# A spectral filter and an MLP on one core: constant tables moved from SyncE's queue into GpSimd's, and four copies and a weight preparation redistributed between two engines

## The chip, the core and the metric

The kernel runs on one core of one Trainium2 chip. The metric is the device time of one execution in microseconds (us); lower is better. The kernel before has a median of 833.29 us over three runs (833.17, 833.29 and 837.02). One further execution was recorded by the profiler; its times are given on their own below.

## What is computed

Eight sequences of 3008 rows with 256 channels are filtered along the rows by a real FFT, a multiplication with a complex filter and the inverse FFT. The 24064 filtered rows then pass through an MLP with 2048 hidden units and the activation h + sin²(alpha·h)/alpha.

```python
# x [8, 3008, 256]; filt_r, filt_i [1505, 256]; w_in [256, 2048]; w_out [2048, 256]
X = np.fft.rfft(x, axis=1)
Y = X * (filt_r + 1j * filt_i)[None]
y = np.fft.irfft(Y, n=3008, axis=1).reshape(24064, 256)
h = y @ w_in
g = h + np.sin(alpha * h) ** 2 / (alpha + 1e-09)
out = g @ w_out
```

## The kernel before, in words

**The transform.** 3008 is 47 times 64, so each transform is two small matrix products with constant tables: a first one over 47 points (table wa), a second one over 64 points (table wb), the product with the filter, and the same two steps backwards with the tables wg (64 points) and we (47 points). All tables are constants of the program and lie in device memory.

**Batches 1 to 7** run woven into the MLP. Their steps (f1, f2x, product, f2g, f3) are put by hand into `plan`, a table of half slots, and between steps the data are reordered by way of device memory, in SyncE's DMA queue. The MLP works on 47 chunks of 512 rows: `mlp_in` (L274), a sine on ScalarE (L276), `square` on VectorE (L281), `mlp_out` (L293), with two `mlp_in` blocks to each of the eight slots of a chunk.

**Batch 0** has nothing to hide behind, so it is done ahead of the MLP, in an order written out by hand (L496 to L505), and reordered on the chip: TensorE multiplies by the identity and the result is copied out of PSUM. Its steps are:

- `f1_chip` (L151): the first forward half; PSUM goes to a_c, half by ScalarE and half by VectorE.
- `turn1` (L162): reorders a_c into bint. `f2x` (L201): the second forward half, with wb; ScalarE copies it to xs.
- `fold_filter` (L405): VectorE copies the filter rows 0 to 63 of fri to rows 64 to 127, 8 of the 24 frequency groups at a time. `product` (L210): VectorE multiplies xs with the two parts of the filter into z and t2, four groups at a time (k = 0 to 5).
- `g_chip` (L172): the first backward half, for one k and one half of the channels: eight matmuls, four of z with wg and four of t2 with a second table, wgs, one after the other in one PSUM tile of 128x512. The copy to b_c is ScalarE's, and VectorE's for the very last tile (k = 5, half 1).
- `turn2` (L183): reorders b_c into gin, two rows at a time. j = 0 to 3 run ahead of the MLP, where ScalarE takes j = 0 and 2 and VectorE 1 and 3; the other twelve lie in the first four slots.
- `f3` (L249): the second backward half into yt, for groups G = 0 and 1 and channel blocks cb = 0 and 1 ahead of the MLP. L264 copies the columns of this chunk, by VectorE for (0, 1) and ScalarE for the other three; L267 copies what belongs to the next chunk, always by VectorE.

z and t2 have two buffers, xs four. PSUM tiles come from three pools: psf (tag f, three), psh (tag ph, three), pso (tag po, two). `keep_busy` (L388) issues matmuls with zeros, so that TensorE isn't idle.

**Loads.** GpSimd issues every transfer that casts float32 to float16, in one queue: x of batch 0 in eight transfers (L134; four parts of 80 and of 14 partitions each), the filter in twelve (L397 and L401: three sets s0 = 0, 8, 16 with two transfers for the real and two for the imaginary part), w_in in four (L479), then x of batch 1 in eight and w_out in two (L348). The first filter transfer waits until part 1 of x has landed. SyncE issues the tables that need no cast, in its own queue, and each waits for a landing:

```python
gate(nc.sync.dma_start(out=wb[:, 8 * 128:], in_=wb_d.ap()[:, 8 * 128:]), x_dma[0, 2])
for s0 in (0, 8, 16):
    cs = slice(128 * s0, 128 * s0 + 1024)
    gate(nc.sync.dma_start(out=wg[:, cs], in_=wg_d.ap()[:, cs]), filter_dma[s0, 0])
    nc.sync.dma_start(out=wgs[:, cs], in_=wgs_d.ap()[:, cs])
```

`filter_dma[s0, 0]` is the second transfer of the real part of set s0. Each piece of wg and of wgs serves two of the six k. The first 8 of the 24 column blocks of wb come early and ungated.

**Weights.** `prep_w_out` (L351) scales the sixteen blocks of w_out by 1/alpha on VectorE, four blocks a call, in slots 6, 8, 10 and 12 of the plan. `mlp_out` of chunk 0 begins in slot 8 and uses the blocks in order.

Of the kernel before, what the change touches and what calls it, by code (L numbers as in the profile page):

```python
# [9 lines left out]
FP16 = mybir.dt.float16  # L10
# [54 lines left out]
def kernel(  # L65
# [10 lines left out]
    nc = tc.nc  # L76
# [51 lines left out]
    def load_x(b, parts=2):  # L128

        xt[b] = (xbpool if b else vpool).tile([GT, RP, C], FP16, name="xt", tag="xb" if b else "vt")  # L130
        n = RP // parts
        for h in range(parts):
            for p0, p1 in ((0, 80), (80, GT)):
                x_dma[b, h] = nc.gpsimd.dma_start(  # L134
                    out=xt[b][p0:p1, n * h:n * h + n, :],
                    in_=dram(x, (b * S + RP * p0 + n * h) * C, [[RP * C, p1 - p0], [1, n * C]]))
# [32 lines left out]
        (nc.vector.tensor_copy if t in (1, 3, 5, 7) else nc.scalar.copy)(  # L169
            out=bint[0][:, 2 * t:2 * t + 2, :], in_=ps)  # L170

    def g_chip(k, half):  # L172

        ps = (psh if half else pso).tile([128, 4, 128], FP32, name="psg0", tag="ph" if half else "po")
        for i in range(4):
            for v, w in ((z, wg), (t2, wgs)):
                nc.tensor.matmul(out=ps[:, i, :], lhsT=v[k][:, i, 128 * half:128 * half + 128],
                                 rhs=w[:, 128 * (4 * k + i):128 * (4 * k + i) + 128],
                                 start=(v is z), stop=(v is t2))
        (nc.vector.tensor_copy if k == 5 and half else nc.scalar.copy)(  # L180
            out=b_c[:, half, :, 4 * k:4 * k + 4, :], in_=ps.rearrange("p s (r a) -> p r s a", a=4))

    def turn2(j):  # L183

        ps = (psf if j < 4 else pso).tile([4 * NK, 2, C], FP32, name="pst2", tag="f" if j < 4 else "po")
        rows = b_c.rearrange("p h r s a -> p h r (s a)")
        for i in range(2):
            for half in range(2):
                nc.tensor.matmul(out=ps[:, i, 128 * half:128 * half + 128],
                                 lhsT=rows[:, half, 2 * j + i], rhs=ident, start=True, stop=True)  # L190
        (nc.scalar.copy if j in (0, 2) or j > 4 and j % 3 == 1 else nc.vector.tensor_copy)(  # L191
            out=gin[0][:, 2 * j:2 * j + 2, :], in_=ps)

    def shuffle1(b):
# [54 lines left out]
    def f3(G, cb):  # L249


        b, a = divmod(G, 8)
        g, lo = divmod(GT * G, 128)
        n = min(GT, 128 - lo)
        if cb == 0:
            if lo == 0 or G == 0:
                yt[g] = ypool.tile([128, 2, 4, 128], FP16, name="yt", tag="yt")
            if n < GT:
                yt[g + 1] = ypool.tile([128, 2, 4, 128], FP16, name="yt", tag="yt")
        ps = psf.tile([128, 4, GT], FP32, name="psy", tag="f")  # L260
        for t in range(4):
            nc.tensor.matmul(out=ps[:, t, :], lhsT=gin[b][:, 4 * a + t, 128 * cb:128 * cb + 128],  # L262
                             rhs=we if b else we2, start=True, stop=True)
        (nc.vector.tensor_copy if G == 0 and cb else nc.scalar.copy)(  # L264
            out=yt[g][:, cb, :, lo:lo + n], in_=ps[:, :, 0:n])
        if n < GT:
            nc.vector.tensor_copy(out=yt[g + 1][:, cb, :, 0:GT - n], in_=ps[:, :, n:GT])  # L267
# [81 lines left out]
                                   in_=moe_w_out[1024 * h:1024 * h + 1024, :].rearrange("(b p) c -> p b c", p=128))  # L349

    def prep_w_out(k):  # L351
        for i in range(4 * k, 4 * k + 4):
            nc.vector.tensor_scalar(out=w_out2[:, i, :], in0=w_out16[:, i, :],  # L353
                                    scalar1=recip[:, i:i + 1], scalar2=None, op0=ALU.mult)

# [59 lines left out]
    def at(slot, f, *args):  # L415
        plan.setdefault(int(2 * slot), []).append((f, args))
# [19 lines left out]
    for g in range(NCH - 1):  # L436
# [4 lines left out]
        slots = (4, 6) if len(todo) == 2 else (3, 4, 6, 7) if g == 4 else (3, 4, 5, 6)  # L441
        for q, u in zip(slots, todo):
            at(8 * g + q, f3, *u)
    for k in range(4):
        at(6 + 2 * k, prep_w_out, k)
    for k in range(2):
        at(13, prep_m, k)
    at(14, load_w_in32, 0)
# [10 lines left out]
    with tc.manual_schedule():  # L459
        nc.sync.dma_start(out=wa2, in_=wa2_d.ap())  # L460
        nc.sync.dma_start(out=ident, in_=id_d.ap())
        nc.scalar.dma_start(out=alpha_r, in_=moe_alpha.rearrange("(a p) -> a p", p=128))
        nc.scalar.dma_start(out=ident32, in_=id32_d.ap())
        nc.scalar.dma_start(out=we2, in_=we2_d.ap())
        nc.scalar.dma_start(out=wa, in_=wa_d.ap())
        nc.scalar.dma_start(out=we, in_=we_d.ap())
        nc.sync.dma_start(out=wb[:, 0:8 * 128], in_=wb_d.ap()[:, 0:8 * 128])
        zero = cpool.tile([128, 512], FP16, name="zero")
        nc.vector.memset(zero, 0.0)
        warm = cpool.tile([128, 1], FP32, name="warm")  # L470
        nc.vector.memset(warm, 0.0)
        nc.scalar.activation(out=warm, in_=warm, func=AFT.Sin)
        load_x(0, 4)
        for s0 in (0, 8, 16):
            load_filter(s0, 8, None if s0 else x_dma[0, 1])
        for h in range(2):
            hs = slice(1024 * h, 1024 * h + 1024)
            for cb in range(2):
                w_in_dma[h, cb] = nc.gpsimd.dma_start(out=w_in16[:, cb, hs],  # L479
                                                      in_=moe_w_in[128 * cb:128 * cb + 128, hs])  # L480
        wgs = ginpool.tile([128, NK * 128], FP16, name="wgs", tag="gin")
        gate(nc.sync.dma_start(out=wb[:, 8 * 128:], in_=wb_d.ap()[:, 8 * 128:]), x_dma[0, 2])
        for s0 in (0, 8, 16):
            cs = slice(128 * s0, 128 * s0 + 1024)
            gate(nc.sync.dma_start(out=wg[:, cs], in_=wg_d.ap()[:, cs]), filter_dma[s0, 0])
            nc.sync.dma_start(out=wgs[:, cs], in_=wgs_d.ap()[:, cs])
        a_c = vpool.tile([128, 2, NK, 128], FP16, name="a_c", tag="vt")
        prep_alpha()
        keep_busy(8, zero)
        for k in range(8):  # L490
            f1_chip(k)
            if k % 2:
                keep_busy(2 if k < 7 else 1, zero)
        bint[0] = xbpool.tile([128, NK, C], FP16, name="bint", tag="xb")
        b_c = agpool.tile([128, 2, RP, NK, 4], FP16, name="b_c", tag="ag")
        for f, *args in (  # L496
                (turn1, 0), (turn1, 1), (turn1, 2), (f2x, 0, 0), (turn1, 3), (turn1, 4), (f2x, 0, 1),
                (turn1, 5), (turn1, 6), (f2x, 0, 2), (turn1, 7), (fold_filter, 0, 8), (turn1, 8),
                (f2x, 0, 3), (product, 0, 0, 0), (turn1, 9), (f2x, 0, 4), (turn1, 10), (f2x, 0, 5),
                (product, 0, 1, 0), (turn1, 11), (f2x, 0, 6), (keep_busy, 2, zero), (g_chip, 0, 0), (g_chip, 0, 1), (f2x, 0, 7),  # L500
                (fold_filter, 8, 8), (f2x, 0, 8), (keep_busy, 2, zero), (product, 0, 2, 0), (g_chip, 1, 0), (g_chip, 1, 1),
                (f2x, 0, 9), (keep_busy, 2, zero), (product, 0, 3, 0), (f2x, 0, 10), (f2x, 0, 11), (keep_busy, 2, zero), (g_chip, 2, 0), (g_chip, 2, 1),
                (fold_filter, 16, 8), (keep_busy, 2, zero), (product, 0, 4, 0), (g_chip, 3, 0), (g_chip, 3, 1),
                (product, 0, 5, 0), (keep_busy, 2, zero), (g_chip, 4, 0), (g_chip, 4, 1), (keep_busy, 2, zero), (g_chip, 5, 0), (g_chip, 5, 1),
                (keep_busy, 1, zero)):  # L505
            f(*args)
        gin[0] = ginpool.tile([4 * NK, RP, C], FP16, name="gin", tag="gin")
        for j in range(4):
            turn2(j)
        load_x(1, 4)  # L510
        load_w_out(0)
        load_w_out(1)
        for i in range(4):
            if i % 2 == 0:
                keep_busy(1, zero)
            f3(i // 2, i % 2)

        for g in range(NCH):
            for q in range(8):
                if g and q == 7:  # L520
                    evict_out(g - 1, 0)
                mlp_in(g, 2 * q)
                if g:
                    mlp_out(g - 1, q, 1)
                for f, args in plan.get(16 * g + 2 * q, ()):
                    f(*args)
                mlp_in(g, 2 * q + 1)
                if g:
                    mlp_out(g - 1, q, 0)
                for f, args in plan.get(16 * g + 2 * q + 1, ()):  # L530
                    f(*args)
                if g and q == 7:
                    evict_out(g - 1, 1)
                    store_out(g - 1, 0, 4, (nc.sync,))
                if q % 2:
                    square(g, q)
        out_last(NCH - 1)
# [28 lines left out]
```

## Time and profile before

| what | value |
|---|---|
| median of three runs | 833.29 us (833.17, 833.29, 837.02) |
| the profiled execution | 836.87 us, of which the span of instructions is 835.0 us |
| TensorE (PE) busy | 816.3 us, 98% of the span |
| VectorE (DVE), ScalarE (ACT), GpSimd (POOL) busy | 509.9, 619.0 and 35.0 us |
| PE busy from 120 to 800 us | 680.0 of 680 us |
| PE busy from 0 to 50 us | 36.9 of 50 us |
| last copy into b_c (batch 0) ends | 39.31 us |
| first mlp_in matmul | 42.23 us |
| mean granted clock of TensorE | 0.998 |

Times within the profile count from the start of the span. A row of the timeline names start and length, the engine, the line of the kernel and what is written from what; in square brackets stands how long the engine was idle before and what ended that wait. A row of the chain of waits names start, length and the piece of work which the end of the program hangs on. The queue q0 (software_dynamic) is the one that GpSimd issues, q1 (hardware_dynamic) the one of SyncE and ScalarE.

### The profile page before, as it was taken

Reading aid. Unit: us, or ns where it says so; the run is one execution under the profiler, and the core shown is the slowest. Engines: PE = TensorE matmul, PEld = TensorE weight load, DVE = VectorE, ACT = ScalarE, POOL = GpSimd, SP = SyncE. Lnnn points to the kernel's source line nnn. Section 1 sums busy time; section 2 is a strip of 40 time slices with the busy share of each in tenths; the row PEclk is TensorE's granted clock in tenths of the full one; section 3 lists DMA queues with packets and bytes.
Section 4 is the critical chain, followed back from the end, with each engine's and each line's share of the span. In section 5 each row is a group of like instructions: output and inputs, shape, how many; then the busy total and the mean of one; then the engine's idle time right before and its main releaser. Section 6 shows DMA issues by size and latency. Waiting matters only on the chain.

```text
span 835.0 us, 15131 instructions
## 1 busy us (share of the span) xinstructions
PE 816.3 (98%) x6242; PEld 573.1 (69%) x6242; DVE 509.9 (61%) x675; ACT 619.0 (74%) x1156; POOL 35.0 (4%) x65
## 2 busy tenths in 40 slices
PE   7699999999999999999999999999999999999997
PEld 4557776677767776677767776677766777766666
DVE  4586976676466665566655684567655775444442
ACT  5596987787777777788777887777877787766663
POOL 5400000000000000000000000000000000000000
PEclk9999999999999999999999999999999999999999
DMA  9946365424543164612834146331645123310111
GB/s 198 210 75 215 120 169 127 141 76 107 145 107 122 51 156 95 202 31 72 191 99 140 51 105 172 101 102 51 160 118 142 61 93 95 67 51 26 26 52 51
DMA packets 67829, 91.28 MB, mean 109 GB/s; under 512 B 5512, under 2 KB 52376, under 8 KB 66248
## 3 DMA queue, kind: packets, MB, share of 16 engines
q1 hardware_dynamic: 59664, 70.99, 29.5%
q0 software_dynamic: 7568, 19.14, 11.8%
q8 instruction: 49, 0.80, 0.4%
q10 hardware_dynamic: 528, 0.18, 0.1%
q14 instruction: 20, 0.16, 0.1%
HBM read 59.62 MB, written 46.66 MB: 127 GB/s over the span
## 4 chain that ended last, share of the span: by engine, by line
PE 91%; DMA 3%; DVE 3%; ACT 1%; POOL 1%; issue 0%; SPq 0%; POOLq 0%; DVEq 0%
PE po L293 42%; PE ph L274 37%; PE psa L143 3%; PE psy L262 3%; PE psg L234 2%; PE psx L204 2%; DMA fri<-in_filt_r_dram 1%; DMA wgs<-wgs_tbl 1%; PE pe L307 1%; DMA xt<-in_x_dram 1%; DVE vt L281 1%; PE psm L372 0%; ACT vt L276 0%; DVE gin L191 0%; DVE w_ina L385 0%
## 5 line engine op out<-in xcount | busy, mean ns | idle before, releaser
L276 ACT ACTIVATE vt<-ph 128x512 f16<-128x512 f32 x688 | 404.5, 601 | 141.8 <-PE ph L274 136.9
L293 PE MATMUL po<-w_out,vt 128*128 128x256 f16 x2944 | 426.5, 272 | 1.1 <-DVE w_out L353 0.6
L293 PEld LDWEIGHTS <-vt 128*128 128x128 f16 x2944 | 287.4, 98 | 172.2 <-issue 1.1
L274 PE MATMUL ph<-yt,w_ina 128*128 128x512 f16 x1376 | 399.4, 379 | 0.0
L281 DVE TENSOR_TENSOR vt<-vt 128x2048 f16<-128x2048 f16 x188 | 230.1, 1224 | 195.3 <-ACT vt L276 194.4
L274 PEld LDWEIGHTS <-w_ina 128*128 128x128 f16 x1376 | 128.2, 98 | 32.6
L318 DVE COPY ot<-po 128x512 f32<-128x512 f32 x92 | 62.9, 688 | 22.2 <-PE po L293 21.3
L208 ACT CAST xs<-psx 128x512 f16<-128x512 f32 x96 | 56.8, 596 | 7.6 <-PE psx L204 7.4
L144 DVE CAST asb<-psa 96x512 f16<-96x512 f32 x56 | 38.3, 685 | 33.4 <-PE psa L143 30.6
L236 ACT CAST gsb<-psg 128x512 f16<-128x512 f32 x84 | 49.5, 589 | 11.5 <-PE psg L234 10.7
L293 PE MATMUL po<-m_t,yt 128*128 128x256 f16 x368 | 55.2, 273 | 0.0
L267 DVE CAST yt<-psy 128x240 f16<-128x240 f32 (+45 forms) x92 | 32.2, 351 | 32.8 <-ACT yt L264 31.6
L264 ACT CAST yt<-psy 128x376 f16<-128x376 f32 (+46 forms) x127 | 45.9, 362 | 7.5 <-PE psy L262 0.6
L276 ACT ACTIVATE vt<-ph,alpha_t 128x512 f16<-128x512 f32 x64 | 43.7, 703 | 9.4 <-PE ph L274 9.3
L262 PE MATMUL psy<-we,gin 96*128 96x94 f16 x512 | 42.1, 204 | 0.0
L134 POOL DMA_DIRECT2D xt<-in_x_dram x40 | 21.3, 540 | 491.8 <-PE psy L262 300.7
L262 PEld LDWEIGHTS <-gin 96*128 96x128 f16 x512 | 35.6, 97 | 6.9 <-issue 0.5
L293 PEld LDWEIGHTS <-yt 128*128 128x128 f16 x368 | 36.0, 98 | 4.2
L144 ACT CAST asb<-psa 96x512 f16<-96x512 f32 x56 | 32.9, 587 | 8.0 <-PE psa L143 7.7
L217 DVE TENSOR_TENSOR z<-xs,fri 128x1024 f16<-128x1024 f16 x48 | 33.0, 687 | 8.3 <-ACT xs L208 4.6
L274 PE MATMUL ph<-yt,w_in 128*128 128x512 f16 x128 | 37.8, 379 | 0.2 <-ACT yt L264 0.2
L204 PE MATMUL psx<-bint,wb 128*128 128x256 f16 x192 | 36.8, 276 | 0.4 <-ACT bint L169 0.2
(69 smaller groups left out, 383.7 us busy)
## 6 DMA issues: line engine op xcount, KB each, us to landing
scr<-asb SPq DMA_DIRECT2D x14, 768.0 KB
bint<-scr SPq DMA_DIRECT2D x21, 512.0 KB
scr<-gsb SPq DMA_DIRECT2D x21, 512.0 KB
out_dram<-ot SPq DMA_DIRECT2D x31, 320.0 KB
xt<-in_x_dram POOLq DMA_DIRECT2D x12, 640.0 KB, 7.7
gin<-scr SPq DMA_DIRECT2D x7, 768.0 KB
out_dram<-ot SPq DMA_DIRECT2D x16, 256.0 KB
gin<-scr SPq DMA_DIRECT2D x7, 576.0 KB
```

The costliest lines, as they stand in the source:

```text
L144: (nc.vector.tensor_copy if u % 2 else nc.scalar.copy)(out=asb[b][:, 2 * u:2 * u + 2, :], in_=ps)
L204: nc.tensor.matmul(out=ps[:, i, :], lhsT=wb[:, 128 * (2 * t + i):128 * (2 * t + i) + 128], rhs=bint[b][:, 2 * t + i, :], start=True, stop= ...
L208: nc.scalar.copy(out=xs[b, t // 2][:, t % 2 * 2:t % 2 * 2 + 2, :], in_=ps)
L217: nc.vector.tensor_tensor(out=z[k], in0=xs[b, k], in1=fri[:, 0, k4, :], op=ALU.mult)
L236: nc.scalar.copy(out=gsb[b][:, 2 * t:2 * t + 2, :], in_=ps)
L262: nc.tensor.matmul(out=ps[:, t, :], lhsT=gin[b][:, 4 * a + t, 128 * cb:128 * cb + 128], rhs=we if b else we2, start=True, stop=True)
L264: (nc.vector.tensor_copy if G == 0 and cb else nc.scalar.copy)(out=yt[g][:, cb, :, lo:lo + n], in_=ps[:, :, 0:n])
L274: nc.tensor.matmul(out=ph, lhsT=(w_in16 if g < 4 else w_ina)[:, cb, 128 * jb:128 * jb + 128], rhs=yt[g][:, cb], start=(cb == 0), stop=(cb ...
L276: nc.scalar.activation(out=vt[g][:, jb, :], in_=ph, func=AFT.Sin, scale=alpha_t[:, jb:jb + 1] if g < 4 else 1.0)
L281: nc.vector.tensor_tensor(out=v4, in0=v4, in1=v4, op=ALU.mult)
L293: nc.tensor.matmul(out=po[g, h][:, i, :], lhsT=vt[g][:, k, ts] if k < 16 else yt[g][:, k - 16, t], rhs=w_out2[:, k, :] if k < 16 else m_t[ ...
L318: nc.vector.tensor_copy(out=ot[g][:, 2 * h:2 * h + 2, :], in_=po[g, h])
```

## The change

It makes five edits.

1. The seven late tables (the rest of wb, three pieces of wg and three of wgs) are issued by GpSimd instead of SyncE, without gates, each set right behind the filter set of the same s0. w_in is issued behind all of them.
2. The last backward tile of batch 0, `g_chip(5, 1)`, becomes two PSUM tiles of two blocks each; VectorE copies the first and ScalarE the second. One of the two zero matmuls ahead of `g_chip(5, 0)` goes.
3. `turn2` with j = 3 is copied by ScalarE, so that ScalarE has three of the first four and VectorE one.
4. The main copies of `f3` ahead of the MLP alternate: VectorE has cb = 0 of both groups, ScalarE cb = 1.
5. `prep_w_out` handles two blocks a call in eight calls, in slots 6, 6.75, 7.5 and so on to 11.25.

```diff
-    def g_chip(k, half):
+    def g_chip(k, half, i0=0, n=4, act=True):
         ps = (psh if half else pso).tile([128, 4, 128], FP32, name="psg0", tag="ph" if half else "po")
-        for i in range(4):
+        for i in range(i0, i0 + n):
...
-        (nc.vector.tensor_copy if k == 5 and half else nc.scalar.copy)(
-            out=b_c[:, half, :, 4 * k:4 * k + 4, :], in_=ps.rearrange("p s (r a) -> p r s a", a=4))
+        (nc.scalar.copy if act else nc.vector.tensor_copy)(
+            out=b_c[:, half, :, 4 * k + i0:4 * k + i0 + n, :],
+            in_=ps[:, 0:n].rearrange("p s (r a) -> p r s a", a=4))
...
-        (nc.scalar.copy if j in (0, 2) or j > 4 and j % 3 == 1 else nc.vector.tensor_copy)(
+        (nc.scalar.copy if j in (0, 2, 3) or j > 4 and j % 3 == 1 else nc.vector.tensor_copy)(
...
-        (nc.vector.tensor_copy if G == 0 and cb else nc.scalar.copy)(
+        (nc.vector.tensor_copy if G < 2 and cb == 0 else nc.scalar.copy)(
...
-        for i in range(4 * k, 4 * k + 4):
+        for i in range(2 * k, 2 * k + 2):
...
-    for k in range(4):
-        at(6 + 2 * k, prep_w_out, k)
+    for k in range(8):
+        at(6 + 0.75 * k, prep_w_out, k)
...
+        wgs = ginpool.tile([128, NK * 128], FP16, name="wgs", tag="gin")
         for s0 in (0, 8, 16):
+            cs = slice(128 * s0, 128 * s0 + 1024)
             load_filter(s0, 8, None if s0 else x_dma[0, 1])
+            if s0 == 0:
+                nc.gpsimd.dma_start(out=wb[:, 8 * 128:], in_=wb_d.ap()[:, 8 * 128:])
+            nc.gpsimd.dma_start(out=wg[:, cs], in_=wg_d.ap()[:, cs])
+            nc.gpsimd.dma_start(out=wgs[:, cs], in_=wgs_d.ap()[:, cs])
...
-        gate(nc.sync.dma_start(out=wb[:, 8 * 128:], in_=wb_d.ap()[:, 8 * 128:]), x_dma[0, 2])
-        for s0 in (0, 8, 16):
-            cs = slice(128 * s0, 128 * s0 + 1024)
-            gate(nc.sync.dma_start(out=wg[:, cs], in_=wg_d.ap()[:, cs]), filter_dma[s0, 0])
-            nc.sync.dma_start(out=wgs[:, cs], in_=wgs_d.ap()[:, cs])
...
-(product, 0, 5, 0), (keep_busy, 2, zero), (g_chip, 4, 0), (g_chip, 4, 1), (keep_busy, 2, zero), (g_chip, 5, 0), (g_chip, 5, 1),
+(product, 0, 5, 0), (keep_busy, 2, zero), (g_chip, 4, 0), (g_chip, 4, 1), (keep_busy, 1, zero), (g_chip, 5, 0), (g_chip, 5, 1, 0, 2, False), (g_chip, 5, 1, 2, 2),
```

More of the change, by code (lines that the diff above doesn't have):

```diff
@@ L170, in turn1 @@
             out=bint[0][:, 2 * t:2 * t + 2, :], in_=ps)
-    def g_chip(k, half):
+    def g_chip(k, half, i0=0, n=4, act=True):
         ps = (psh if half else pso).tile([128, 4, 128], FP32, name="psg0", tag="ph" if half else "po")
-        for i in range(4):
+        for i in range(i0, i0 + n):
             for v, w in ((z, wg), (t2, wgs)):
-                nc.tensor.matmul(out=ps[:, i, :], lhsT=v[k][:, i, 128 * half:128 * half + 128],
+                nc.tensor.matmul(out=ps[:, i - i0, :], lhsT=v[k][:, i, 128 * half:128 * half + 128],
                                  rhs=w[:, 128 * (4 * k + i):128 * (4 * k + i) + 128],
                                  start=(v is z), stop=(v is t2))
-        (nc.vector.tensor_copy if k == 5 and half else nc.scalar.copy)(
-            out=b_c[:, half, :, 4 * k:4 * k + 4, :], in_=ps.rearrange("p s (r a) -> p r s a", a=4))
+        (nc.scalar.copy if act else nc.vector.tensor_copy)(
+            out=b_c[:, half, :, 4 * k + i0:4 * k + i0 + n, :],
+            in_=ps[:, 0:n].rearrange("p s (r a) -> p r s a", a=4))
     def turn2(j):
@@ L480 @@
                                                       in_=moe_w_in[128 * cb:128 * cb + 128, hs])
-        wgs = ginpool.tile([128, NK * 128], FP16, name="wgs", tag="gin")
-        gate(nc.sync.dma_start(out=wb[:, 8 * 128:], in_=wb_d.ap()[:, 8 * 128:]), x_dma[0, 2])
-        for s0 in (0, 8, 16):
-            cs = slice(128 * s0, 128 * s0 + 1024)
-            gate(nc.sync.dma_start(out=wg[:, cs], in_=wg_d.ap()[:, cs]), filter_dma[s0, 0])
-            nc.sync.dma_start(out=wgs[:, cs], in_=wgs_d.ap()[:, cs])
         a_c = vpool.tile([128, 2, NK, 128], FP16, name="a_c", tag="vt")
```

## The prediction

> **What bounds the kernel now.** I first read the page's busy times and slices.
>
> ```profile
> span 835.0 us, 15131 instructions
> ...
> PE 816.3 (98%) x6242; PEld 573.1 (69%) x6242; DVE 509.9 (61%) x675; ACT 619.0 (74%) x1156; POOL 35.0 (4%) x65
> ...
> PE   7699999999999999999999999999999999999997
> ...
> DMA  9946365424543164612834146331645123310111
> ```
>
> TensorE idles for 18.7 us in all. The table of windows says where: 13.1 us of it before 50 us, 4.3 us in the last 35, none from 120 to 800. The change touches only the first 70 us, so what it is worth is how much earlier the MLP starts, and all behind that shifts with it. Hence the chain of waits for the first 70 us:
>
> ```profile
> 14.44 10.77 DMA fri<-in_filt_r_dram
> 25.21 0.02 issue
> 25.23 0.32 SPq L485
> 25.55 0.05 issue
> 25.60 10.61 DMA wgs<-wgs_tbl
> 36.20 0.04 issue
> 36.24 1.00 PE psg L177 x15
> ...
> 38.61 0.70 DVE b_c L180
> ```
>
> From 14 to 36 us two transfers follow each other: a filter load of 10.8 us, whose landing lets SyncE issue the last wg and wgs, which takes 10.6 us more. 256 KB in 10.6 us is slow, so something else ran beside it. The waits of the same window say that it is always wgs, and GpSimd's timeline says what ran beside it:
>
> ```profile
> PE psg L177 <- DMA wgs<-wgs_tbl: 4.8, 3, 1.9
> ...
> 19.57 1.21 POOL L401 DMA_DIRECT2D fri<-in_filt_i_dram  x1 [1.96 <-DMA fri<-in_filt_i_dram]
> 20.76 0.56 POOL L479 DMA_DIRECT2D w_in<-in_moe_w_in_dram  x1
> 22.71 1.06 POOL L479 DMA_DIRECT2D w_in<-in_moe_w_in_dram  x2 [1.39 <-DMA fri<-in_filt_r_dram]
> 24.10 1.18 POOL L479 DMA_DIRECT2D w_in<-in_moe_w_in_dram  x1 [0.33 <-DMA fri<-in_filt_i_dram]
> 29.25 4.19 POOL L134 DMA_DIRECT2D xt<-in_x_dram  x7 [3.97 <-PE idle L392]
> ```
>
> All of w_in (needed at 42 us) and the start of x of batch 1 (needed at 51 us) are in the DMA engines ahead of or beside the tables needed at 30 to 36 us. The DMA share of the windows is 1.0 to 1.4 from 5 to 45 us: the engines are full, and order is all there is to gain. GpSimd's waits also show a limit: the issue at 22.71 waits for the landing of the real part of filter set 8, as SyncE's gated issue at 22.44 does. That is the eighth transfer before it, so eight are in flight.
>
> **Edit 1, the queue.** I work out when things land if served strictly in the order issued. Prices are the packet records of this trace (packets of both queues, median): 322 ns for 4096 bytes with cast, 60 ns for 512 bytes with cast, 84 ns for 2048 and 159 ns for 4096 bytes of a table; 16 engines share them. A filter set is two transfers of 32 packets of 4096 and two of 256 of 512: (64 x 322 + 512 x 60) / 16 = 3.2 us. The rest of wb is 128 x 159 / 16 = 1.3 us, a piece of wg or wgs 128 x 84 / 16 = 0.67 us. x of batch 0 has landed at 13.05 us (TensorE's last wait for it). Up to the end of the third filter set come 3 x 3.2 + 1.3 + 4 x 0.67 = 13.6 us: 26.6 us. The records in fact run slower at times: from 13.05 to 23.92 (fold of set 8 released) 9.1 us of packets took 10.9; from there to 36.6 (first x of batch 1 landed) 13.1 took 12.7; together 6% over. So filter set 16 lands at 13.05 + 13.6 x 1.06 = 27.5, the last wgs 1.4 us later at 29.
>
> What is late then? VectorE, from the landing of set 16: fold 1.14, product 4 and 5 at 4 x 0.61, 0.08 to the end of the last, together 3.66 us; 15 matmuls at 0.055 and 0.2 to the result; a copy of 0.36 (ScalarE's 272 columns took 0.39): 5.1 us, and the last b_c ends at 32.6 instead of 39.31. There is a floor: VectorE comes free from turn1 at 18.2 and has three folds and twelve products, 3 x 1.14 + 12 x 0.61 + 0.08 = 10.8 us, ending at 29.0; with 1.4 us for matmuls and copy, 30.4. ScalarE (16 copies at 0.48 from 22 us) would end at 29.8, near but not behind it. The same in-order walk with before's landings gives 39.2 for the measured 39.31.
>
> GpSimd gets seven issues more, 7 x 0.55 = 3.9 us. It idles as much before, 2 us each ahead of the issues at 17.11 and 19.57, and behind the seven stand only w_in and x of batch 1. With eight transfers in flight (some 6 us of packets) the issuing stays ahead; without that cover it would cost its 3.9 us. w_in lands some 5.8 us behind the tables, first half at about 32, and is needed at 42.23 - 8 = 34. x of batch 1 (needed 50.85 - 8 = 43) and w_out (first half needed at 56.09 - 8 = 48; landed at about 44 to 47 before) have the same bytes ahead of them as before, so they land when they did: 1 to 4 us of cover remain.
>
> **What the trace doesn't show** is a table issued by GpSimd. Lower end: 84 ns as in SyncE's queue; upper end: w_in's packet of the same size with its cast, 172 ns. A table has no cast, so I take 84. No packet of the trace moves its bytes faster, so nothing below that.
>
> Beside the rows: the fold at 19.40 (1.22 us) and the issue at 19.57, which took 1.21 instead of 0.58, end together, and so for 23.94 and 24.10; the products don't do this (0.56 at 20.76 beside one). The Trainium skill, SBUF — State Buffer, section "SBUF: two separate sides", has a rule against this change: GpSimd can't write descriptors while VectorE holds the port pair they share, and a plain load belongs in another engine's queue. The trace agrees for the folds.
>
> **Edits 2 to 5.** The last tile in halves and one zero matmul less: without edit 1 a copy of 0.69 becomes 0.36 and 0.22 us goes, some 0.4 us; it is inside the 5.1 and 1.4 above. turn2(3): VectorE ends it at 41.49, ScalarE could at 40.39 + 0.38 + 0.59 = 41.36. f3: VectorE's slower copy (0.54 for ScalarE's 0.47) stands against the one moved off VectorE; the first mlp_in comes 0 to 0.3 earlier; I take 0.15. prep_w_out: the pieces are due earlier and 0.4 instead of 0.8 us long. TensorE waits 0.59 for the last one (at 70.03) and 0.27 for an asb copy that stood behind four of them (57.60). VectorE is full from 50 to 60 us, so some of that comes back elsewhere: between a loss of 0.3 and a gain of 0.6, I take 0.3.
>
> **The sum.** The profiled execution took 836.87. With set 16 at 27.5: 836.87 - (39.31 - 32.6) - 0.45 = 829.7. But two of three timed runs took 833.2, 3.7 less than the profiled one and the third. TensorE has no idle time from 120 to 800 us to lose 3.7 in, so I put the difference into the landings of the start. If they are 3.6 us quicker over the 23.2 us from 13.05 to the last wgs (a factor of 0.85), set 16 lands at 25.3 and the b_c ends at 30.4, the floor: 836.87 - 8.9 - 0.45 = 827.5. Two of three runs are of that kind, so the median should be. I forecast **827.7**, 5.6 under the median. If the 3.7 lie elsewhere, the shift of 7.2 comes off 833.2: 826.
>
> **Rivals.**
> - *Table packets at the cast price.* All seven at twice the price: 1.3 + 4 x 0.7 = 4.1 us up to set 16, 1.4 more to the last wgs: 34.4; from there 2.6 us to the b_c (39.31 - 36.22 less 0.45): 37.0. That gives 836.87 - 2.3 - 0.45 = 834.1, 832 for the quicker kind. For it: no such packet in the trace; against: nothing to cast. 8%.
> - *GpSimd held up by VectorE.* Each of three folds holds an issue for 0.6 us, and landings slip by 1.9 us at most: 827.7 + 1.9 = 829.6. The Trainium skill's rule (above) would work here in this way. Against: the queue is eight deep. 6%.
> - *Given back later.* The MLP starts 8 us earlier, but w_out or x of batch 1 comes when it came; one that is 3 us later than before holds VectorE's queue and then TensorE: 830 to 832. 7%.
> - *Slower.* The tables' rows are cut into packets of 512 bytes, as the filter's reversed rows and w_out's are. Then the 1.57 MB ahead of set 16 take 3072 x 60 / 16 = 11.5 us instead of 4.1, and the last two pieces 3.8 us: the last wgs lands at 27.5 + 7.4 + 3.8 = 38.7 instead of 36.2, the start is 2 us later, and w_in and w_out land some 10 us later, at up to 57, where 48 to 56 is needed: 838 to 843. It would show as 4096 packets of 512 bytes more in q0 for the 896 of the tables; below half of that the start is still earlier than before. Against: x's contiguous rows go in 4096-byte packets. 5%.
> - *My forecast*, 825.3 to 830: 74%.
>
> Over 0.5% (4.2 us, about what a measurement of this kernel can tell from no change) faster means below 829.1: four fifths of the forecast and a third of the second rival, 0.61. Slower by as much: 0.05. Within: 0.34. The range of 8 in 10 reaches from 825 (826 with the full 0.6 of edits 3 to 5 and early landings) to 832, which takes in the first three rivals' lower parts.
>
> **What would show it.** Right: no wait of psg for wg or wgs; the last b_c between 30 and 33 us; set 16's fold the last wait for a DMA; VectorE busy almost without gaps from 18 to 29; w_in issued behind 20 us; the first mlp_in at 33 to 36. Wrong: packets of q0 up by thousands; waits for w_in, w_out or xt behind 33 us; TensorE idle between 40 and 70 us by more than the 2 us of before; the granted clock at half while TensorE is on the chain (from 23 to 27 us the windows show 0.56 to 0.59, after TensorE had idled from 21 to 23).

## The result and the profile after

The changed kernel takes 830.21 us (median of 11 runs, 828.93 to 833.66); the kernel before took 834.02 in 11 runs beside them (832.81 to 838.09). The ratio is 0.9943, with a 95% interval from 0.9926 to 0.9960: 3.3 to 6.2 us faster. The profiled execution took 830.46 us, against 836.87 before.

First the page of the changed kernel, the span, TensorE's slices and the DMA queues.

```profile
span 828.6 us, 15125 instructions
...
PE   7899999999999999999999999999999999999997
...
q1 hardware_dynamic: 58656, 68.90, 29.0%
q0 software_dynamic: 8192, 21.24, 12.8%
```

The reader is to see that the start has one fuller slice, and that 2.1 MB went from q1 to q0. q0 has 624 packets more (8192 for 7568), not thousands: the tables were not cut up but went in 512 packets of 4096 bytes. Next, from the chain of waits of the first 60 us (start, length, piece of work):

```profile
15.45 8.57 DMA fri<-in_filt_i_dram
...
24.21 1.23 DVE fri L408
```

The 10.6 us of wgs are gone from the chain. What is left is the last transfer of filter set 8 (0.24 us of issue, then 8.57 to its landing) and VectorE's fold of it. VectorE's timeline shows what follows:

```profile
24.21 1.22 DVE L408 COPY fri<-fri 64x4096 f16<-64x4096 f16 x1 [1.75 <-DMA fri<-in_filt_i_dram]
...
28.10 1.23 DVE L408 COPY fri<-fri 64x4096 f16<-64x4096 f16 x1
...
31.28 0.69 DVE L220 TENSOR_TENSOR t<-xs,fri 128x1024 f16<-128x1024 f16 x1
32.85 0.42 DVE L180 CAST b_c<-psg 128x256 f16<-128x256 f32 x1 [0.88 <-PE psg L177]
```

ScalarE's last copies into b_c (four in one row) and the first mlp_in matmul:

```profile
31.41 2.07 ACT L180 CAST b_c<-psg 128x512 f16<-128x512 f32 x4 [1.50 <-PE psg L177]
...
36.34 0.71 PE L275 MATMUL ph<-yt,w_in 128*128 128x512 f16 x2
```

Set 8 keeps VectorE waiting 1.75 us. From there it works without a gap to the last product; set 16 has landed (27.88) when VectorE gets to it at 28.10. The last copy into b_c (ScalarE's half) ends at 33.48 instead of 39.31, and the first mlp_in matmul starts at 36.34 instead of 42.23: 5.9 of the 6.4 us between the two profiled executions. TensorE's waits in the 30 us behind that are shorter as well. Before (window 42 to 72), then after (36 to 66):

```profile
PE po L293 <- DVE w_out L353: 0.6, 1, 0.6
PE pst L189 <- DVE gin L191: 0.4, 2, 0.2
PE psa L143 <- DVE asb L144: 0.3, 1, 0.3
PE ph L274 <- ACT yt L264: 0.2, 1, 0.2
```

```profile
PE pst L190 <- DVE gin L192: 0.4, 2, 0.2
```

### The profile page after: what moved, and what is told of

It reads as the page before. It is cut to its first block, busy times and chain, and to the rows that moved or that the text cites. A ratio compares the mean times of both kernels' runs of the same rounds, so it can differ in the third digit from the quotient of the medians.

```text
span 828.6 us, 15125 instructions
## 1 busy us (share of the span) xinstructions
PE 814.0 (98%) x6241; PEld 570.9 (69%) x6241; DVE 509.0 (61%) x675; ACT 619.1 (75%) x1157; POOL 38.7 (5%) x72
## 3 DMA queue, kind: packets, MB, share of 16 engines
q0 software_dynamic: 8192, 21.24, 12.8%
## 4 chain that ended last, share of the span: by engine, by line
PE 93%; DVE 3%; DMA 2%; POOL 1%; ACT 1%; issue 1%; DVEq 0%; POOLq 0%
PE po L294 43%; PE ph L275 38%; PE psa L143 3%; PE psy L263 3%; PE psg L235 2%; PE psx L205 2%; DMA fri<-in_filt_i_dram 1%; PE pe L308 1%; DMA xt<-in_x_dram 1%; DVE vt L282 1%; PE psm L373 0%; PE psg L177 0%; ACT vt L277 0%; PE pst L190 0%; DVE w_ina L386 0%
## 5 line engine op out<-in xcount | busy, mean ns | idle before, releaser
L268 DVE CAST yt<-psy 128x240 f16<-128x240 f32 (+45 forms) x92 | 32.3, 351 | 32.7 <-ACT yt L265 31.4
L265 ACT CAST yt<-psy 128x376 f16<-128x376 f32 (+45 forms) x126 | 45.7, 363 | 7.2 <-PE psy L263 0.3
```

The source lines that it names most:

```text
L265: (nc.vector.tensor_copy if G < 2 and cb == 0 else nc.scalar.copy)(out=yt[g][:, cb, :, lo:lo + n], in_=ps[:, :, 0:n])
```

## The experiments

The theory going in: the order of the transfers decides when the tables and filter sets land, and the landing sets the start of the MLP. The rivals were that edits 2 to 5 carry half of the gain, that GpSimd's queue as such (not the order) brings it, and that something else now bounds the start. Ratios below are to the kernel before, run beside each kernel on the same chip, with 95% intervals.

| kernel | ratio | last b_c copy, first mlp_in in its profile (us) |
|---|---|---|
| changed | 0.9943 (0.9926 to 0.9960) | 33.5, 36.34 |
| edit 1 alone | 0.9962 (0.9945 to 0.9978) | 32.7, 35.66 |
| edits 2 to 5 alone | 0.9998 (0.9981 to 1.0015) | 37.7, 40.54 |
| before, w_in held | 0.9976 (0.9963 to 0.9990) | 34.6, 37.52 |
| changed, wb in halves | 0.9954 (0.9938 to 0.9970) | 33.8, 36.62 |
| changed, 512 KB more ahead of set 16 | 0.9978 (0.9958 to 0.9997) | 34.2, 37.34 |
| changed, 512 KB more behind the tables | 0.9944 (0.9924 to 0.9964) | 33.0, 35.83 |
| changed, filter rows read forward | 0.9937 (0.9918 to 0.9957) | 34.2, 37.06 |
| changed order, SyncE's queue | 0.9941 (0.9922 to 0.9960) | 32.8, 35.64 |
| changed, fold on two engines | 0.9965 (0.9947 to 0.9984) | 34.5, 37.43 |

**The two halves of the change.** First edit 1 alone: the kernel before with the loop of the changed one that issues filter and tables.

> Kernel before with edit 1 alone. Theory (the order of the transfers sets the start; after the change it is the landing of filter set 8, at 24.0 us, plus VectorE's unbroken row of two folds and eight products): set 8 lands at 23.5 to 24.5 us, the last copy into b_c ends at 33.5 to 34.3 us, and the time is 0.3 to 1.0 us above the changed kernel, 830.5 to 831.2. Rival (edits 2 to 5 carry half of the gain): 832 or more.

Then the rest alone: the changed kernel with the old loop and SyncE's gated tables.

> Kernel before with edits 2 to 5, tables still in SyncE's queue. Theory: the last wgs lands where it did, 32 to 36.5 us, last copy into b_c 2.6 us behind it, the wait of 0.59 us for w_out at 70 us is gone; time 0.3 to 1.0 us under the kernel before, 833.0 to 833.7. Rival (edits 2 to 5 carry half of the gain): 832 or less. If the last wgs lands well before 36 us in this profile, the profile of the kernel before was of one of its later landings, which is where I put the 3.7 us between its runs.

Edit 1 alone gives 0.9962, the rest alone 0.9998 with an interval that reaches to either side of 1. Edit 1 carries most of the gain, two thirds by the middle of the intervals; "half each" falls. The two parts add up to 0.0040 of 0.0057; the intervals leave room for that difference, and no run here explains it. In the profile of the rest alone the last copy into b_c ends at 37.7, and the tables are again what TensorE waits for (total, times, longest):

```profile
PE psg L177 <- DMA wg<-wg_tbl: 3.1, 2, 2.2
...
PE psg L177 <- DMA wgs<-wgs_tbl: 2.1, 2, 1.4
```

In that of edit 1 alone it ends at 32.7, earlier than expected, and set 16, not set 8, is what VectorE waited for last:

```profile
22.73 1.22 DVE L407 COPY fri<-fri 64x4096 f16<-64x4096 f16 x1
...
26.95 1.22 DVE L407 COPY fri<-fri 64x4096 f16<-64x4096 f16 x1 [0.36 <-DMA fri<-in_filt_i_dram]
```

The order of the landings is the same as in the changed kernel, but set 8 landed 1.9 us earlier here (22.09 for 24.02). Which of the two sets binds differs between executions.

**Is it w_in?** In the kernel before, one wait is added, so that w_in isn't issued beside the tables.

```diff
                 w_in_dma[h, cb] = nc.gpsimd.dma_start(...)
+                if h == 0 and cb == 0:
+                    gate(w_in_dma[h, cb], filter_dma[16, 1])
```

> Kernel before with one wait added: w_in is issued only when the last filter transfer (set 16) has landed; tables stay in SyncE's queue with their gates. Theory (w_in beside the tables is what made them late): the last wgs lands at 28 to 31 us, last copy into b_c at 33 to 34.5 us, time 830 to 832. Rival (the queue or the gates as such, not w_in): last wgs within 1.5 us of the kernel before, time within 0.7 us of it.

0.9976: w_in's place alone gives a part of the gain, two fifths by the middle of the intervals. The last wgs landed at 28.92 and is no longer waited for. What is left over shows in TensorE's timeline of this kernel, where the first pieces of wg and wgs are still late:

```profile
21.60 0.22 PE L177 MATMUL psg<-wg,z 128*128 128x128 f16 x1 [0.76 <-DMA wg<-wg_tbl]
23.34 0.27 PE L177 MATMUL psg<-wgs,t 128*128 128x128 f16 x1 [1.53 <-DMA wgs<-wgs_tbl]
```

Piece 0 of wgs is issued behind a gate at set 0 and shares the DMA engines with filter sets 8 and 16, which are needed later than it. VectorE then has to wait for z's buffers.

**Is it the queue or the order?** Here the tables go back to SyncE, with gates one step earlier, and w_in is held.

```diff
-            if s0 == 0:
-                nc.gpsimd.dma_start(out=wb[:, 8 * 128:], ...)
-            nc.gpsimd.dma_start(out=wg[:, cs], ...)
-            nc.gpsimd.dma_start(out=wgs[:, cs], ...)
...
+        gate(nc.sync.dma_start(out=wb[:, 8 * 128:], ...), x_dma[0, 2])
+        for s0, earlier in ((0, x_dma[0, 3]), (8, filter_dma[0, 1]), (16, filter_dma[8, 1])):
+            gate(nc.sync.dma_start(out=wg[:, cs], ...), earlier)
+            nc.sync.dma_start(out=wgs[:, cs], ...)
...
+                if h == 0 and cb == 0:
+                    gate(w_in_dma[h, cb], filter_dma[16, 0])
```

> Changed kernel with the tables back in SyncE's queue, but with gates one step earlier than before (wg and wgs of set 0 behind the last x, of set 8 behind filter set 0, of set 16 behind filter set 8), and w_in held until the real part of filter set 16 has landed. Theory (it is the order of the transfers, and the queue doesn't matter): last copy into b_c at 32.5 to 34.5 us, time 830 to 831.3. Rival (GpSimd's queue as such brings the gain, tables in a second queue are served in turn with what should come first): 832.5 or more, as with w_in held alone.

0.9941, the same as the changed kernel. Against edits 2 to 5 alone (0.9998) only the gates and w_in's wait differ; the tables come by SyncE's queue in both. So which engine issues the tables makes no measurable difference; when they come in relation to filter and w_in does. One queue is a simple way to write the order down, since it needs no gates.

**What bounds the start now.** A useless transfer of 512 KB, first ahead of filter set 16, then behind the last wgs:

```diff
             cs = slice(128 * s0, 128 * s0 + 1024)
+            if s0 == 16:
+                nc.gpsimd.dma_start(out=w_out16[:, 0:8, :].rearrange("p b c -> p (b c)"), in_=wb_d.ap()[:, 0:2048])
             load_filter(s0, 8, None if s0 else x_dma[0, 1])
```

> Changed kernel with a useless transfer of 512 KB (columns of wb into the room where w_out comes later) issued right ahead of filter set 16. Theory (the start is bound by the landings of the filter sets, and so by the bytes ahead of them): set 16 lands 1.3 us (packet price) to 1.9 us (what the rest of wb took) later, the last copy into b_c ends at 34.5 to 35.5 us, time 831.5 to 832.2. Rival (VectorE's own row of folds and products bounds the start, with landings ahead of it): time within 0.4 us of the changed kernel.

> Changed kernel with the same useless transfer right behind the last wgs, ahead of w_in. Theory (only what lies ahead of the tables and filters counts; w_in, x of batch 1 and w_out have cover): time within 0.4 us of the changed kernel, though all later loads land 1.3 to 1.9 us later. Rival (given back later: the later loads are the next bound): 831.5 or more, with waits for w_in or w_out.

Ahead of set 16 the ratio rises from 0.9943 to 0.9978, 2.9 us, with intervals that barely touch; behind the tables it stays (0.9944). That is more than the 1.3 to 1.9 us that I had expected and than this profile shows (its first mlp_in comes 1.0 us later than in the first profile of the changed kernel). So landings bind, and w_in, x of batch 1 and w_out have cover: no late wait came in place of the one removed. In the profile with the transfer ahead, set 8 came early and VectorE's longest wait is for set 16:

```profile
22.47 1.22 DVE L408 COPY fri<-fri 64x4096 f16<-64x4096 f16 x1
...
28.03 1.22 DVE L408 COPY fri<-fri 64x4096 f16<-64x4096 f16 x1 [1.70 <-DMA fri<-in_filt_i_dram]
```

Then two tries to bring the landings forward. In the first, half of the rest of wb stands behind set 8.

```diff
-                nc.gpsimd.dma_start(out=wb[:, 8 * 128:], in_=wb_d.ap()[:, 8 * 128:])
+                nc.gpsimd.dma_start(out=wb[:, 8 * 128:16 * 128], in_=wb_d.ap()[:, 8 * 128:16 * 128])
+            if s0 == 8:
+                nc.gpsimd.dma_start(out=wb[:, 16 * 128:], in_=wb_d.ap()[:, 16 * 128:])
```

> Changed kernel with the rest of wb in two transfers: columns 8 to 15 where they are, columns 16 to 23 behind filter set 8. Theory (set 8 sets the start): set 8 lands 0.9 us earlier, near 23.1 us, the last copy into b_c ends near 32.4 us instead of 33.5, time 0.9 us under the changed kernel, about 829.3. Rival (something else than set 8 bounds the start, so its earlier landing is idle): last copy into b_c at 33.2 to 33.5 us, same time within 0.3 us.

My theory for this one was too narrow. Set 8 was folded at 23.58 instead of 24.21, but then VectorE waited 0.89 us for set 16, which landed at 28.24, and the last b_c copy came at 33.8. Set 16 has the same bytes ahead of it in either order, so a gain at set 8 alone would be given back there. The trace marks each landing in sixteen steps. Fifteen of those of set 8 had come by 20.85 us, against 22.48 in the first profile of the changed kernel; the last came at 23.39, against 24.02. So the bytes ahead seem to count for most of the set, and one late step kept much of that gain from VectorE. The second try takes packets away: the second half of each filter transfer is read in forward order. These rows then stand in the wrong order, so this kernel tells of the time alone.

```diff
-                in_=dram(src, (MT - s0) * C, [[MT * C, 32], [-C, n], [1, C]]))
+                in_=dram(src, (MT - s0 - n + 1) * C, [[MT * C, 32], [C, n], [1, C]]))
```

> Changed kernel with the second half of each filter transfer read in forward order, so that 256 packets of 512 bytes become 32 of 4096; the rows of the filter are then in the wrong order, everything else is computed as before. Theory (landings bind): 0.3 us less for each of two transfers a set by packet price, so set 8 lands 1.2 us and set 16 1.9 us earlier; last copy into b_c at 31 to 32.3 us, time 828.3 to 829.3. Rival (VectorE's row, which would end at 30.4 us without waits, is already the bound): within 0.4 us of the changed kernel.

The time doesn't move measurably (0.9937 for 0.9943), though 1536 packets of 512 bytes became 192 of 4096. In this profile the sets landed at 23.12 and 28.72, where the two profiles of the changed kernel have 24.02 and 27.88, and 22.62 and 27.33 (the second of them is below):

```profile
23.31 1.22 DVE L408 COPY fri<-fri 64x4096 f16<-64x4096 f16 x1 [0.86 <-DMA fri<-in_filt_i_dram]
...
28.75 1.30 DVE L408 COPY fri<-fri 64x4096 f16<-64x4096 f16 x1 [1.59 <-DMA fri<-in_filt_i_dram]
```

VectorE waits for both sets here, so the rival that I had named (VectorE's own row already the bound) isn't what this shows either. It is the price by packet that falls: it had set 16 landing 1.9 us earlier, and even the eighth of the sixteen steps of that landing came at 25.27, against 26.16 and 25.48. The windows of the changed kernel suggest a better price (the last column is GB/s as written; 9 to 11 is x in large packets, 15 to 17 the tables, 43 to 45 w_out in 512-byte packets):

```profile
9.00:11.00 2.00, 1.27 (x18) 0.81 (x18) 1.05 (x3) 0.86 (x2) 1.24 (x3) 1.00 1.05 206
15.00:17.00 2.00, 1.71 (x24) 1.42 (x22) 1.38 (x3) 1.97 (x4) 1.36 (x3) 1.00 1.04 344
43.00:45.00 2.00, 1.78 (x17) 1.26 (x17) 1.53 (x3) 1.70 (x3) 0.00 (x0) 1.00 1.35 181
```

Cast data arrive at about 200 KB a us in packets of either size, tables at 344. With the cast two bytes are read for one written, so the reading goes at 340 to 410 KB a us throughout. The number of packets doesn't set the pace; that the bytes read do fits these rows, but no run tests it by itself.

**VectorE's row behind the last landing.** The fold of set 16 is shared: ScalarE copies the imaginary part, and VectorE multiplies both z ahead of both t2.

```diff
+        if s0 < 16:
+            nc.vector.tensor_copy(out=fri[64:128, :, s0:s0 + n, :], in_=fri[0:64, :, s0:s0 + n, :])
+            return
+        nc.vector.tensor_copy(out=fri[64:128, 0, s0:s0 + n, :], in_=fri[0:64, 0, s0:s0 + n, :])
+        nc.scalar.copy(out=fri[64:128, 1, s0:s0 + n, :], in_=fri[0:64, 1, s0:s0 + n, :])
```

> Changed kernel, where the fold of filter set 16 is shared: VectorE copies the real part, ScalarE the imaginary part, and VectorE multiplies z of k = 4 and 5 ahead of t2 of k = 4 and 5, so that ScalarE has the time. Theory (VectorE's row behind the last landing is on the path): from the fold's start to the end of the last t2 3.1 us instead of 3.9, start 0.5 to 0.6 us earlier for the same landing; time 829.5 to 830, too little to be told by the time alone, so the profile decides. Rival (ScalarE's copies into b_c, which stand behind its part of the fold, are late then): last copy into b_c no earlier against the landing, 5.2 us or more.

The rival is right. ScalarE comes to its part of the fold only when its copies into b_c are done, at 28.03, takes 1.90 us for what VectorE does in 0.69, and VectorE waits for it:

```profile
28.03 1.90 ACT L416 COPY fri<-fri 64x2048 f16<-64x2048 f16 x1
```

```profile
29.96 0.69 DVE L222 TENSOR_TENSOR t<-xs,fri 128x1024 f16<-128x1024 f16 x1 [1.33 <-ACT fri L416]
```

From the start of the fold to the last t2 it is 4.8 us instead of 3.9. No version beat the changed kernel measurably.

**Edit 5 alone taken back** (the changed kernel with w_out prepared in fours):

> Changed kernel without edit 5: w_out prepared four blocks a call in slots 6, 8, 10 and 12 again. Theory (edit 5 alone took TensorE's two waits away): TensorE idles 0.86 us between 10 and 30 us behind the first mlp_in, in the same two waits (0.3 for an asb copy, 0.6 for w_out), where the changed kernel idles 0.00. Rival (the transfers or edits 3 and 4 took them away): 0.00 to 0.3.

Both waits are back (0.6 for w_out, 0.3 for asb). The windows from 10 to 30 us behind the first mlp_in, of the second profile of the changed kernel (below) and of this one:

```profile
45.59:65.59 20.00, 20.00 (x160) 13.51 (x159) 17.80 (x38) 17.83 (x34) 0.00 (x0) 1.00 0.31 81
```

```profile
49.45:69.45 20.00, 19.14 (x151) 12.61 (x150) 17.55 (x38) 17.93 (x34) 0.00 (x0) 1.00 0.31 80
```

TensorE is busy 20.00 and 19.14 of 20 us: in this stretch edit 5 is worth 0.86 us. Over all that follows the start (time less the start of mlp_in) it is 795.2 here and 794.1 in the changed kernel, but 794.5 and 794.6 in the two profiles of the kernel before, which lacks edit 5 as well: 0.4 to 1.1 us. This execution took 834.61 mostly because its filter sets landed late (folds at 24.75 and 29.85), and the last wgs with them.

**The same kernels once more.** One further profile each of the kernel before and of the changed one.

> The kernel before, unchanged, profiled once more. Theory (what differs between two executions of one program is when the last transfers of a row land, and only the start sees it): the last wgs lands anywhere from 33 to 37.5 us, and the execution's time less the start of the first mlp_in matmul is 794.6 us give or take 0.5, as in the first profile (836.87 - 42.23). Rival (the difference between executions lies behind the start): the first mlp_in at 42.2 give or take 0.5, whatever the time.

> The changed kernel, unchanged, profiled once more. Theory (as for the kernel before): filter set 8 or set 16 lands up to 1.5 us earlier or later than in the first profile, the last copy into b_c ends 9.2 us behind the landing of set 8 or 5.2 us behind that of set 16, whichever is later, and the time less the start of the first mlp_in is 794.1 give or take 0.5. Rival: first mlp_in at 36.3 give or take 0.3.

The kernel before took 832.40 this time. Its last wait for wgs and its first mlp_in:

```profile
31.87 0.22 PE L177 MATMUL psg<-wgs,t 128*128 128x128 f16 x1 [1.37 <-DMA wgs<-wgs_tbl]
...
37.86 0.59 PE L274 MATMUL ph<-yt,w_in 128*128 128x512 f16 x2 [0.19 <-ACT yt L264]
```

That is 4.4 us earlier than in the first profile for both, and 4.5 us in the whole time (836.87 to 832.40). The changed kernel took 829.69, with its first mlp_in at 35.59 instead of 36.34. In all profiles the time less the start of mlp_in is 794.1 to 795.6 us. The executions of one program differ in when the last transfers land, and the rest of the kernel passes that on. The last wgs landed at 31.83, outside the 33 to 37.5 that I had expected, and in the first profile at 36.20. Fifteen of its sixteen steps had come by 31.80 here and by 33.20 there: 3.0 of the 4.4 us are one late step. In the second profile of the changed kernel both sets made VectorE wait a little:

```profile
22.81 1.22 DVE L408 COPY fri<-fri 64x4096 f16<-64x4096 f16 x1 [0.16 <-DMA fri<-in_filt_i_dram]
...
27.36 1.22 DVE L408 COPY fri<-fri 64x4096 f16<-64x4096 f16 x1 [0.69 <-DMA fri<-in_filt_i_dram]
```

## Why the prediction was right or wrong, point by point

- **What bounds the kernel: right.** The tables, late because w_in shared the DMA engines with them, set the start, and the MLP passes it on. Holding w_in alone gives two fifths of the gain, edit 1 alone two thirds; the difference between these two I put down to the order of the first pieces of the tables, but their intervals overlap. Of the signs that I named, the last b_c copy (30 to 33) and the first mlp_in (33 to 36) came at 33.48 and 36.34 in the first profile, just outside, and at 32.73 and 35.59 in the second.
- **Landing of set 16 at 27.5: right in its value, not in its working.** It landed at 27.88 in the first profile, 27.33 in the second, 26.93 with edit 1 alone. The price by packet (3.2 us a set) was too high: at 200 KB a us a set of 524 KB takes 2.6. Against that I had nearly nothing for the stragglers. In the three profiles the eighth of the sixteen steps of set 16's last transfer came at 26.16, 25.48 and 25.10, and the last 1.7 to 1.9 us later; with the rows read forward it was 3.45 us. The two errors cancel, and that is luck.
- **5.1 us from set 16 to the last b_c copy: right, 0.3 short.** 5.4 from the start of the fold in the second profile (27.36 to 32.7).
- **Which wait is last: half right.** Set 16 in some executions, set 8 in others. The sum gave set 8 no landing of its own; by its prices and its 6% it would have been 22.6. In the first profile it landed at 24.02 and was folded at 24.21, and 9.3 us lie from there to the last b_c copy.
- **The step from 829.7 to 827.7: wrong.** I was right that the 3.7 us between runs of the kernel before lie in the landings (the last wgs at 31.8 in one execution, 36.2 in the other). The failing step is that I scaled all landings by 0.85, so that set 16 would come at 25.3 and VectorE's row without waits (30.4) become the bound. But in the two profiled executions of the kernel before, of 832.40 and 836.87, set 16 landed at the same time (26.45 and 26.39): what varied was the last wgs, which the change takes out of the path. The row without waits was too low as well. VectorE was free for it at 18.6, not 18.2, and a fold with its four products took 3.9 us (24.21 to 28.10), not 3.6, so that without any wait the last b_c copy would have ended at 31.8, not 30.4 (18.6, three times 3.9, and 1.5 for the matmuls and the copy). The forecast of 827.7 is also 0.2 above the 827.5 of its own sum, without a reason. The sum for the profiled execution, 829.7, was within 0.8 us of what its profile then gave (830.46), and the median is 830.21. Its terms came out at 5.8 us for the last b_c copy, where 6.7 was expected, and at 0.6 for edits 3 to 5, where it had 0.45.
- **Edits 2 to 5.** Edit 2: from the end of the last t2 to the last b_c copy it is 1.92 us in the profile of edit 1 alone and 1.51 after, 0.4 as predicted. Edits 3 and 4: from the last b_c copy to the first mlp_in 2.92 before, 2.86 after; 0.15 was expected, 0.06 came. Edit 5: 0.86 where I took 0.3 from a range that ended at 0.6. I had feared that VectorE, full in these slots, would give it back; it did not in that stretch, but only 0.4 to 1.1 us show in the whole, and in two profiles (edits 2 to 5 alone, rows read forward) TensorE waited 0.7 and 1.1 us for a yt copy later on. These gains are too small for the timed runs, which give the four edits together 0.9998.
- **Rivals.** Table packets at the cast price: no; the tables moved at 344 GB/s. Cut into 512 bytes: no; they went in 4096-byte packets of 159 ns, a little cheaper by byte than the 84 ns for 2048 that I had held to be the least. Given back later: no; an extra 512 KB ahead of w_in cost nothing. GpSimd held up by VectorE: the issue of the last wgs at 24.37 took 1.19 us beside the fold at 24.21, but nothing waited for that. The Trainium skill, SBUF — State Buffer, section "SBUF: two separate sides", would have plain loads moved away from GpSimd for this lock; here the tables in SyncE's queue (with gates in the order of need) and in GpSimd's gave 0.9941 and 0.9943.

## What to carry to other kernels

Where the DMA engines are full, write down the bytes in the order in which they are needed, and let nothing that is needed later share them; one queue does that without gates. Work out landings from the rate that the windows show for each kind of transfer, add the stragglers, and look at each landing that feeds the engine which is last, not only at the final one. When runs of one program differ, find out which landing varies before you scale all of them: take the rest of the kernel off each profiled time and see whether it is constant.

## What the runs showed of the hardware that was not expected

- With the cast, 512-byte and 4096-byte packets arrive at about the same rate (181 and 206 GB/s written), though a packet's own time (60 and 322 ns) makes the small ones look half again as dear per byte. A DMA share of 1.35 in the row 43 to 45, more than all 16 engines' time, says that packets overlap.
- The last landing of one and the same row of transfers differs by 4.4 us between two executions where two queues share the engines (36.20 and 31.83), and 3.0 of this is the last of its sixteen steps. With one queue the stragglers stay: set 8 landed at 24.02 and 22.62 in the changed kernel, and at 24.56 in the version without edit 5, each time 2.0 to 3.1 us behind the eighth step. What makes them the runs don't show.
- ScalarE takes 1.90 us for a 64x2048 copy between fp16 tiles, VectorE 0.69 for the same.
